# Merging two DMA transposes into one, moving four more transposes to DMA, and splitting the last eviction, in a fused recurrence and two-layer kernel

## The chip, the cores and the metric

The kernel runs on one core of a Trainium2 chip. The metric is the device time of one execution in microseconds (us). Three runs of the kernel before gave 184.88, 185.29 and 185.72 us, median 185.29 us. The profile was taken of a separate execution of 186.47 us, in which the span from the first to the last recorded instruction is 184.7 us.

Five engines are named as the profile names them: PE (matrix multiply, with PEld for its weight loads), DVE, ACT, POOL and SP. SP does no arithmetic. It issues most of the DMAs, one after another, in the order written in the program.

## The reference

Two steps follow one another. The first is a gated linear recurrence for 4 batches, 8 heads, 768 time steps and a head dimension of 48, the second is a two-layer network over the 3072 tokens that the first step gives.

```python
B, H, S, D = q.shape                     # 4, 8, 768, 48
for t in range(S):
    state = alpha[:, :, t, :, None] * state + np.einsum('bhd,bhe->bhde', k[:, :, t], v[:, :, t])
    y[:, :, t] = np.einsum('bhd,bhde->bhe', q[:, :, t], state)
x = y.transpose(0, 2, 1, 3).reshape(B * S, H * D)   # 3072 x 384
h = x @ w_in                             # 384 x 2048
g = np.maximum(h, 0.0) ** 2
out = g @ w_out                          # 2048 x 384
```

## The kernel before

**Tiling.** The 3072 tokens are cut into 24 chunks of 128 time steps, six for each batch. A chunk is a 128 x 384 tile of x once its recurrence is done. The chunks are numbered from 0, so chunk 14 is the 15th.

**Recurrence of a chunk.** The loop over time steps is replaced by matrix products inside a chunk and a state carried from chunk to chunk. For chunk s the steps are: the logarithm of alpha (`e_ln`, ACT); its running sums in two layouts (`e_p0` and `e_pT`, PE); exponentials of these (ACT); products of the exponentials with q and k (DVE); the scores (`e_p2`, PE); a mask (`e_sm`, DVE); the state update (`e_ps`, PE, and `e_stm`, `e_sb`); and the chunk's y in two parts (`e_p3a`, `e_p3b`, PE). `e_xn` (ACT, line 615) copies y out of PSUM as the bf16 tile `xn`.

**Two ways to transpose q and k.** Up to chunk 10 the products are transposed on PE. From chunk `RAW = 11` on, q and k themselves are cast to bf16 on POOL into `rawb` (`e_rb`, line 415) and transposed by a DMA into `rawt` (`e_turn`, line 418): one DMA for q and one for k. `e_qAT` (DVE, line 509) reads the q half of `rawt`, `e_kz` (line 513) the k half, and the scores need both. `rawb` and `rawt` have `NR = 3` slots.

**Two ways to transpose x.** The second step needs x with its columns on the partitions, in `xT_big`. `e_p4` (PE, three transposes) with `e_xT` (DVE copy, line 390 through `cast`) does it for most chunks. For chunks in `XTURN = (18, 23)`, that is 18 to 22, a DMA transposes `xn` straight into `xT_big` (`e_xt`, line 625). Chunk 23 goes through PE again.

**The two-layer step.** Groups of tokens (`GN`: 4, 1, 1, then two chunks each) go through `add_moe1` (x times w_in, relu on ACT, square on DVE) and `add_moe2` (times w_out, four quarters of four matmuls for each chunk). The first matmul of a pair such as chunks 14 and 15 reads `xT_big` of both. The result leaves PSUM by `e_ev` (ACT or DVE) and goes to memory by a DMA that SP issues, or for chunks 8 to 17 by one that POOL issues; chunks 0 to 7 are held and stored in two large DMAs late.

**What sets the order.** A planner (`Plan.run`) runs in Python while the program is built. Each piece of work is an `Op` with an engine, an assumed duration, a latency and what it depends on; the planner places them one by one and then emits the instructions in the order of the assumed starts. The order on every engine is therefore fixed in the program: PE, SP and POOL run their lists strictly one after another, and an instruction that must wait holds up all those behind it on the same engine. The planner's pseudo-engines "DMA", "TR" and "OUT" all become SP's one list: loads, transposes and stores. Its constants `LD1`, `TLD`, `TLAT`, `TLATE` say how long it assumes a load or a transpose to take. `gate` holds back the recurrence of chunk s until the two-layer step has come within `LEAD = 3.5` chunks of it.

**SP's list around the change.** Loads are written Q, K, V, A (for q, k, v, alpha), the q and k transposes Tq and Tk, the x transposes X, each with its chunk. Before the change the part that matters reads: Q12 Tq11 K12 Tk11 V12 A14 Tq12 Q13 K13 Tk12 V13 A15 Q14 Tq13 K14 Tk13 V14 A16 Q15 Tq14 K15 Tk14 V15 A17 Q16 Tq15 K16 Tk15 V16 A18 Tq16 Q17 Tk16 K17 V17 A19 Q18 Tq17 K18 Tk17 V18 Tq18 A20 Q19 Tk18 K19 V19 A21 Q20 Tq19 K20 Tk19 V20 Tq20 A22 Q21 Tk20 K21 X18 V21 A23 Tq21 Q22 Tk21 K22 V22 X19 Tq22 Q23 Tk22 K23 X20 V23 Tq23 Tk23 X21, two large stores, X22, and the last stores.

Lines that the steps touch:

Of the kernel before, what the change touches and what calls it, by code (L numbers as in the profile page):

```python
# [8 lines left out]
FP32 = mybir.dt.float32  # L9
# [45 lines left out]
def after(op, x=0.0):  # L55
    return (op, x)
# [85 lines left out]
def kernel(  # L142
# [10 lines left out]
    nc = tc.nc  # L153
    B, H, S, D = q.shape
    HD = H * D
    P = 128
# [3 lines left out]
    d_model, d_ff = moe_w_in.shape  # L160
# [3 lines left out]
    NT = n_tok // P  # L164
# [13 lines left out]
    opool = ctx.enter_context(tc.tile_pool(name="opool", bufs=6))  # L178
# [15 lines left out]
        out=utri_f, in_=utri_f, compare_op=ALU.is_ge, fill=0.0,  # L194
# [10 lines left out]
    for c in range(JN):  # L205
        blk = slice(JP * c, JP * c + JP)
        nc.gpsimd.affine_select(
            out=tri4[blk, 0:JW], in_=tri4[blk, 0:JW], compare_op=ALU.is_ge, fill=0.0,
# [27 lines left out]
    def pin(ins):  # L236
        tc.keep_in_program_order(ins)

    def mm(*a, **kw):
        pin(nc.tensor.matmul(*a, **kw))  # L240

    def tr(*a):
        pin(nc.tensor.transpose(*a))  # L243
# [13 lines left out]
    X_SLACK = 0.2  # L257
    LD = 0.98
    LD1 = 1.0
    WLD = 2.1  # L260
    LAG = 3.2
    SQ_PRIO = 0.0

    def add(eng, dur, emit, *deps, **kw):
        return plan.add(Op(eng, dur, emit, deps, **kw))
# [6 lines left out]
    def load_w(which):  # L272
# [25 lines left out]
        prev = w_cast[-SB] if len(w_cast) >= SB else None  # L298
        ld = add("DMA", WLD * n / 4 + 0.03, e_issue, prev, lat=LAG if which == "o" else 2.0)
        op = add({"POOL": 0.1 + 0.46 * n, "DVE": 0.1 + 0.2 * n, "ACT": 0.1 + 0.32 * n}, 0, e_cast, ld, prio=-3.0)  # L300
# [6 lines left out]
    C = [dict() for _ in range(NT)]  # L307
# [1 line left out]
    SRC = dict(srcs)  # L309
    EARLY = 4  # L310
    RAW = 11
    XTURN = (18, 23)
    TLD, TLAT, TLATE = 1.0, 4.0, 2.0
    NR = 3
    R = {}

# [49 lines left out]
    def add_load(s, nm):  # L366
        d = C[s]
        b, c = divmod(s, NCH)

        def ld():  # L370
            if nm not in d:
                d[nm] = loads.tile([P, H, D], FP32, name=nm)
            pin(nc.sync.dma_start(out=d[nm], in_=SRC[nm][b, c]))
        prev = C[s - LB].get("use_" + nm) if s >= LB else None
        d["ld_" + nm] = add("DMA", LD if s < 4 else LD1, ld, prev, lat=2.0 if s < 4 else LAG if s < 6 else 2.4, at=0.6)

    def add_chunk(s):
        d = C[s]
        b, c = divmod(s, NCH)
# [3 lines left out]
        g = dict(prio=-10.0 + s * 0.01)  # L383
# [26 lines left out]
        if raw:  # L410
            w, wz = s % NR, s % 2

            def e_rb(j, nm):
                raw_tiles()
                pin(nc.gpsimd.tensor_copy(R["b"][:, w, j, :, 0:D], d[nm]))  # L415

            def e_turn(j):
                pin(nc.sync.dma_start_transpose(out=R["t"][:, w, j], in_=R["b"][:, w, j].rearrange("p h d -> p (h d)")))
            rt = []
            for j, nm in enumerate(["qt", "kt"]):  # L420
                cb = add("POOL", 0.55, lambda j=j, nm=nm: e_rb(j, nm), d["ld_" + nm],
                         *([C[s - NR]["turn"][j]] if s >= RAW + NR else []), prio=-5.0)
                d["use_" + nm] = cb
                t_ = add("TR", TLD, lambda j=j: e_turn(j), cb, *([C[s - NR]["turned"][j]] if s >= RAW + NR else []), lat=TLAT)
                t_.late = TLATE
                rt.append(t_)
            d["turn"] = rt
        vb = d["use_vt"] = add("POOL", 0.55, e_vb, d["ld_vt"], old, prio=-5.0)

        def e_p0():  # L430
# [49 lines left out]
        if raw:  # L480
# [8 lines left out]
            aT = add("ACT", 0.48, e_AT, pT, after(ai) if ai else None, **g)  # L489
            aiT = add("ACT", 0.48, e_AiT, pT, after(aT), *([C[s - 2]["p2"]] if s >= RAW + 2 else []), **g)  # L490
# [20 lines left out]
        def e_kz(hh):  # L511
            rows = slice(DP * hh, DP * hh + DP)
            pin(nc.vector.tensor_mul(R["z"][rows, wz, :, hh, :], R["t"][rows, w, 1], R["i"][rows, wz]))  # L513
        if raw:
            if not last:
                mk = d["use_kt"] = add("DVE", 0.47, e_kI, ai, d["ld_kt"], old, **g)
            cp = add("DVE", 0.34, e_qAT, aT, rt[0], **g)
            prz = C[s - 2]["p2"] if s >= RAW + 2 else None
            kz0 = add("DVE", 0.45, lambda: e_kz(0), aiT, rt[1], prz, **g)
            kz1 = add("DVE", 0.45, lambda: e_kz(1), aiT, rt[1], prz, after(kz0), **g)  # L520
            d["turned"] = [cp, kz1]
            cpk = kz1
        else:
            mq = d["use_qt"] = add("DVE", 0.47, e_qA, a_, d["ld_qt"], old, **g)
            mk = d["use_kt"] = add("DVE", 0.47, e_kI, ai, d["ld_kt"], old, **g)
# [13 lines left out]
        def e_cp(lo, hi):  # L539
            if lo == 0:  # L540
                d["qkT"] = work.tile([P, 2 * NP, P], BF16, name="qkT")
            cast(cpk if lo else cp, d["qkT"][:, lo:hi, :], d["pT"][:, lo:hi, :])
        if s < EARLY:
            cp = add({"ACT": 0.49, "DVE": 0.34}, 0, lambda: e_cp(0, NP), p1q, **g)
            cpk = add({"DVE": 0.34, "ACT": 0.49}, 0, lambda: e_cp(NP, 2 * NP), p1k, after(cp, -9.0), **g)
        elif not raw:
            cp = cpk = add("DVE", 0.61, lambda: e_cp(0, 2 * NP), p1k, **g)
# [23 lines left out]
        if not last:  # L571
# [7 lines left out]
            prev = C[s - 1].get("sb") if s else None  # L579
            if c == 0 and s:  # L580
                prev = C[s - 2]["sb"]
# [34 lines left out]
        xn = add("ACT", 0.36, e_xn, p3b, **g)  # L616
        (p3a or p3b).gives = xn

        def e_p4():
            d["px"] = psum(p4, [P, KT, P], BF16)  # L620
            for j in range(KT):
                tr(d["px"][:, j, :], d["xn"][:, j * P:(j + 1) * P], ident_bf)
        if XTURN[0] <= s < XTURN[1]:
            def e_xt():
                pin(nc.sync.dma_start_transpose(out=xT_big[:, :, s * P:(s + 1) * P], in_=d["xn"]))
            d["x"] = add("TR", 0.8, e_xt, xn, lat=TLAT)
            d["x"].late = 1.0
            d["end"] = xn
            return
# [17 lines left out]
    OUT_LATE = 3.5  # L647
# [7 lines left out]
    prog = {"m1": 0.0, "m2": 0.0}  # L655
# [40 lines left out]
    def add_moe2(g, tt, before, box, quarters, pools):  # L696

        for qd in quarters:
            def e_mm(qd=qd):
                if qd == 0:  # L700
                    box["po"] = psum(box["first"], [P, 512], FP32)[:, 0:d_model]
                for kf in range(qd * FT // NQ, (qd + 1) * FT // NQ):
                    mm(box["po"], lhsT=gT[g][:, kf, tt * P:(tt + 1) * P], rhs=w_out_b[:, kf, :],
                       start=(kf == 0), stop=(kf == FT - 1))
            fs = range(qd * FT // NQ, (qd + 1) * FT // NQ) if g == 0 else range(FT)
            deps = [o for f in fs for o in sq[(g, f)]] + [w_dep("o", fs[-1] if g == 0 else FT - 1)] + ([after(before)] if before else [])
            op = plan.add(Op("PE", 0.65, e_mm, deps, takes=pools if qd == 0 else None, prio=0.1))
            op.moe = (2, 2.56 / NQ)
            if qd == 0:
                box["first"] = op  # L710
            op.lat = 0.05
            before = op
        if quarters[-1] < NQ - 1:
            return op

        t = GT[g] + tt
        held = t < HELD

        def e_ev():
            if held:  # L720
                if t % 4 == 0:
                    KEEP[t // 4] = stage.tile([P, 4, d_model], FP32, name="keep", tag="stage")
                box["ob"] = KEEP[t // 4][:, t % 4, :]
            else:
                box["ob"] = opool.tile([P, d_model], FP32, name="ob")
            if ev.eng == "DVE":
                pin(nc.vector.tensor_copy(box["ob"], box["po"]))
            else:
                pin(nc.scalar.copy(box["ob"], box["po"]))  # L729
        ev = add({"DVE": 0.47, "ACT": 0.38}, 0, e_ev, op, prio=-15.0)  # L730
        box["first"].gives = ev

        def e_held():
            pin(nc.sync.dma_start(out=out_r[t - 3:t + 1].rearrange("t p n -> p t n"), in_=KEEP[t // 4]))
        if held:
            held_ev.append(ev)
            if t % 4 == 3:
                add("OUT", 2.2, e_held, *held_ev[-4:], at=HELD_AT)
            return op

        def e_out():
            dma = nc.gpsimd if pool_out else nc.sync
            pin(dma.dma_start(out=out_r[GT[g] + tt], in_=box["ob"]))
        pool_out = POOL_OUT[0] <= GT[g] + tt < POOL_OUT[1]
        if pool_out:
            o = add("POOL", 1.0, e_out, ev, prio=5.0)
            o.late, o.moves = 0.5, 0.5
        else:
            add("OUT", 0.55, e_out, ev, at=0.0).late = OUT_LATE
        return op  # L750

    DMA_ORDER = ["at", (0, "qt"), (0, "kt"), (1, "qt"), (1, "kt"), (0, "vt"), (2, "qt"),
# [51 lines left out]
    LEAD = 3.5  # L804

    def gate(op):
        s = getattr(op, "gla", None)
        if s is not None:
            return s <= LEAD + (prog["m1"] + prog["m2"]) / 5.12
        return True  # L810

    def on_pick(op):
# [15 lines left out]
    for op in plan.order:  # L828
        if op.eng == "PE":
# [3 lines left out]
            if pe_end is not None and DUMMY and not opened and op.start < CALM:  # L833
                n = max(0, int((op.start - pe_end) / 0.11 + (0.4 if op.start < DENSE else -1.8)))
# [35 lines left out]
```

## Time and profile before

| what | value |
|---|---|
| median of three runs | 185.29 us |
| profiled execution, device time | 186.47 us |
| its span | 184.7 us |
| PE busy | 177.7 us, 96% of the span |
| DVE busy, ACT busy | 130.6 us, 126.7 us |
| DMA packets under 512 B | 112384 of 120056 |
| transposes by DMA: q and k, x | 26, 5 |
| transposes of xn on PE | 57 (19 chunks of 3) |

In the profile, "SPq" is SP's list. A line of the timeline gives the start, the duration and what was issued; a DMA's duration there is the time its issue took, not the time until its data arrived. "DMA to landing" is the time from issue to arrival. Line numbers are those of the kernel before; PE's lines are those of two helpers (240 for a matmul, 243 for a transpose), so its work is told apart by tiles.

### The profile page before, as it was taken

The page shows a single profiled execution, that of the slowest core. Times are in us where ns is not written, and L with a number is a line of the kernel's source. Part 1 is how long each engine was busy: PE and PEld are TensorE (multiplying, and loading weights), DVE is VectorE, ACT ScalarE, POOL GpSimd, SP SyncE. Part 2 cuts the span into 40 slices and gives each one's busy share as a digit, 9 for nine tenths or more (in the row PEclk, how much of TensorE's full clock was granted, in tenths as well). Part 3 has the DMA queues.
Part 4 walks back from the last instruction along what each step waited for, and adds up shares of the span by engine and source line. Part 5 has one row for each costly group of instructions (what it writes and reads, how often), then busy time and mean ns, then how long its engine had stood idle before and what let it go on. Part 6 is the DMA issues. An engine that isn't in the chain of part 4 may idle for free.

```text
span 184.7 us, 4919 instructions
## 1 busy us (share of the span) xinstructions
PE 177.7 (96%) x1886; PEld 133.5 (72%) x1886; DVE 130.6 (71%) x283; ACT 126.7 (69%) x288; POOL 41.8 (23%) x81
## 2 busy tenths in 40 slices
PE   7798999999999999999999999999999999999992
PEld 2467795467868887977867867868876877978661
DVE  1248898965899998776878877868866786845100
ACT  3657699606867996958958958958965975848221
POOL 8121100011161134142224242243243311000000
PEclk9969999999999999999999999999999999999999
DMA  5999999999989888989999899999999967601112
GB/s 167 215 216 243 270 367 331 324 233 214 209 169 218 171 173 165 177 155 172 154 168 205 158 196 177 237 186 155 220 164 205 207 97 248 202 4 43 41 47 85
DMA packets 120056, 34.12 MB, mean 185 GB/s; under 512 B 112384, under 2 KB 118784, under 8 KB 120032
## 3 DMA queue, kind: packets, MB, share of 16 engines
q1 hardware_dynamic: 119392, 31.83, 83.6%
q0 software_dynamic: 640, 1.97, 3.1%
q8 instruction: 15, 0.25, 0.6%
q14 instruction: 9, 0.07, 0.2%
HBM read 25.17 MB, written 4.72 MB: 162 GB/s over the span
## 4 chain that ended last, share of the span: by engine, by line
PE 88%; ACT 6%; DMA 2%; issue 1%; DVE 1%; SPq 0%; ACTq 0%
PE bank L240 76%; PE sc L240 5%; PE bank L243 5%; ACT r L681 3%; DMA at<-in_alpha_dram 2%; PE st L240 2%; DVE w_out_b L295 1%; ACT A L464 0%; ACT gT L343 0%; ACT xn L388 0%; ACT Ainv L468 0%; ACT w_in_b L297 0%; ACT qkT L388 0%; ACT L_s L398 0%; ACT ob L729 0%
## 5 line engine op out<-in xcount | busy, mean ns | idle before, releaser
L240 PE MATMUL bank<-xT_big,w_in_b 128*128 128x256 bf16 (+2 forms) x636 | 73.6, 262 | 0.1
L240 PE MATMUL bank<-w_out_b,gT 128*128 128x384 bf16 x384 | 71.1, 326 | 0.5 <-DVE w_out_b L295 0.5
L681 ACT ACTIVATE r<-bank 128x512 bf16<-128x512 f32 x96 | 55.9, 618 | 7.3 <-PE bank L240 6.2
L240 PEld LDWEIGHTS <-w_in_b 128*128 128x128 bf16 x636 | 53.3, 98 | 8.0 <-issue 0.2
L240 PEld LDWEIGHTS <-gT 128*128 128x128 bf16 x400 | 36.0, 98 | 20.1 <-DVE w_out_b L295 1.0
L689 DVE TENSOR_TENSOR gT<-r 128x512 bf16<-128x512 bf16 x96 | 40.9, 455 | 9.6 <-ACT r L681 8.8
L566 DVE TENSOR_TENSOR sm<-sc,utri_b 128x512 bf16<-128x512 f32 x48 | 30.8, 684 | 5.9 <-PE sc L240 5.7
L407 POOL CAST vb<-vt 128x384 bf16<-128x384 f32 x24 | 13.5, 561 | 65.6 <-DMA vt<-in_v_dram 52.2
L729 ACT COPY ob<-bank 128x384 f32<-128x384 f32 x16 | 7.7, 478 | 19.1 <-PE bank L240 18.8
L507 DVE TENSOR_TENSOR kI_s<-kt,Ainv 128x384 bf16<-128x384 f32 x21 | 12.4, 591 | 7.3 <-ACT Ainv L468 7.3
L388 ACT CAST xn<-bank 128x384 bf16<-128x384 f32 x24 | 11.5, 479 | 8.3 <-PE bank L240 8.3
L415 POOL CAST rawb<-qt 128x384 bf16<-128x384 f32 x13 | 8.0, 614 | 19.8 <-DMA qt<-in_q_dram 15.7
L591 ACT CAST sb<-st 128x384 bf16<-128x384 f32 x20 | 9.7, 484 | 3.8 <-DVE st L586 3.6
L586 DVE TENSOR_TENSOR st<-st,ae_s 128x384 f32<-128x384 f32 x20 | 11.2, 559 | 1.5 <-ACT ob L729 0.5
L513 DVE TENSOR_TENSOR kz<-rawt,kz 64x512 bf16<-64x512 bf16 x26 | 11.5, 441 | 1.1 <-ACT kz L456 0.4
L415 POOL CAST rawb<-kt 128x384 bf16<-128x384 f32 x13 | 7.9, 607 | 17.7 <-DMA kt<-in_k_dram 16.5
L240 PE MATMUL bank<-warm 128*128 128x256 bf16 (+1 forms) x48 | 10.5, 356 | 1.3 <-DVE warm L188 1.3
L504 DVE TENSOR_TENSOR qA_s<-qt,A 128x384 bf16<-128x384 f32 x11 | 6.1, 551 | 7.7 <-ACT A L464 7.7
L398 ACT ACTIVATE L_s<-at 128x384 bf16<-128x384 f32 x20 | 10.6, 530 | 0.2
L468 ACT ACTIVATE Ainv<-bank 128x384 bf16<-128x384 f32 x21 | 10.6, 503 | 0.0
L240 PEld LDWEIGHTS <-qkT 64*128 64x128 bf16 (+1 forms) x168 | 7.9, 96 | 3.1 <-issue 0.8
L240 PEld LDWEIGHTS <-sm 128*128 128x128 bf16 x192 | 8.2, 96 | 1.5 <-DVE sm L566 0.2
(65 smaller groups left out, 181.4 us busy)
## 6 DMA issues: line engine op xcount, KB each, us to landing
qt<-in_q_dram SPq DMA_DIRECT2D x24, 192.0 KB, 4.1
kt<-in_k_dram SPq DMA_DIRECT2D x24, 192.0 KB, 3.7
vt<-in_v_dram SPq DMA_DIRECT2D x24, 192.0 KB, 3.8
at<-in_alpha_dram SPq DMA_DIRECT2D x20, 192.0 KB, 3.9
wo<-in_moe_w_out_dram SPq DMA_DIRECT2D x4, 768.0 KB, 8.3
out_dram<-ob POOLq DMA_DIRECT2D x10, 192.0 KB, 3.6
wi<-in_moe_w_in_dram SPq DMA_DIRECT2D x4, 384.0 KB, 5.4
wi<-in_moe_w_in_dram SPq DMA_DIRECT2D x2, 768.0 KB, 7.9
```

The lines of the kernel that those rows point to most:

```text
L240: pin(nc.tensor.matmul(*a, **kw))
L388: pin(nc.scalar.copy(out_t, in_t))
L398: pin(nc.scalar.activation(L[:, :, 0:D], d["at"], AF.Ln))
L407: pin(nc.gpsimd.tensor_copy(d["vb"], d["vt"]))
L415: pin(nc.gpsimd.tensor_copy(R["b"][:, w, j, :, 0:D], d[nm]))
L468: pin(nc.scalar.activation(d["Ai"], d["pm"][:, 0:HD].rearrange("p (h d) -> p h d", h=H), AF.Exp, scale=-1.0))
L507: pin(nc.vector.tensor_mul(kI[:, :, 0:D], d["kt"], d["Ai"]))
L513: pin(nc.vector.tensor_mul(R["z"][rows, wz, :, hh, :], R["t"][rows, w, 1], R["i"][rows, wz]))
L566: pin(nc.vector.tensor_mul(d["sm"][:, hh], d["sc"][:, hh], utri_b.to_broadcast([P, NP, P])))
L586: pin(nc.vector.tensor_mul(st4, st4, bcast(ae, D)))
L681: pin(nc.scalar.activation(box["r"][:, 0:w], box["ph"][:, 0:w], AF.Relu))
L689: pin(nc.vector.tensor_mul(gT[g][:, f0:f0 + per, lo * P:lo * P + n], r, r))
```

## The change

Four things change.

1. `e_turn` no longer takes a chunk's q and k one by one. A single DMA transposes both, 128 x 1024 elements in place of two of 128 x 512. It depends on both casts, and everything that read one half of `rawt` now depends on it. 26 such DMAs become 13.
2. `XTURN` becomes (14, 23): x of chunks 14, 15, 16 and 17 is transposed by DMA too, in place of three PE transposes and one DVE copy each.
3. The planner's constants change: `LD2 = 0.93` for loads from chunk 11 on, `TLD`, `TLAT`, `TLATE`, and the assumed time of an x transpose. `gate` lets the recurrence run up to half a chunk further ahead from chunk 13 on. These change the order only.
4. The last tile's result is copied out of PSUM by DVE (left half) and ACT (right half), and its store waits for both.

SP's list becomes: Q12 K12 T11 V12 A14 Q13 T12 K13 V13 A15 Q14 K14 T13 V14 A16 Q15 T14 K15 V15 A17 Q16 K16 T15 V16 A18 Q17 T16 K17 V17 A19 Q18 T17 K18 X14 V18 A20 Q19 K19 T18 V19 X15 A21 Q20 T19 K20 V20 X16 A22 Q21 T20 K21 V21 X17 A23 Q22 K22 T21 V22 Q23 K23 X18 V23 T22 X19 T23 X20 X21, a large store, X22, the other large store, and the last stores.

```diff
+    LD2 = 0.93
-    XTURN = (18, 23)
-    TLD, TLAT, TLATE = 1.0, 4.0, 2.0
+    XTURN = (14, 23)
+    TLD, TLAT, TLATE = 1.2, 4.5, 1.5
...
-        d["ld_" + nm] = add("DMA", LD if s < 4 else LD1, ld, prev, lat=2.0 if s < 4 else LAG if s < 6 else 2.4, at=0.6)
+        d["ld_" + nm] = add("DMA", LD if s < 4 else LD1 if s < RAW else LD2, ld, prev, lat=2.0 if s < 4 else LAG if s < 6 else 2.4, at=0.6)
...
-            def e_turn(j):
-                pin(nc.sync.dma_start_transpose(out=R["t"][:, w, j], in_=R["b"][:, w, j].rearrange("p h d -> p (h d)")))
+            def e_turn():
+                pin(nc.sync.dma_start_transpose(
+                    out=R["t"][:, w].rearrange("p j n t -> p (j n) t"), in_=R["b"][:, w].rearrange("p j h d -> p (j h d)")))
             rt = []
             for j, nm in enumerate(["qt", "kt"]):
                 cb = add("POOL", 0.55, lambda j=j, nm=nm: e_rb(j, nm), d["ld_" + nm],
-                         *([C[s - NR]["turn"][j]] if s >= RAW + NR else []), prio=-5.0)
+                         C[s - NR]["turn"] if s >= RAW + NR else None, prio=-5.0)
                 d["use_" + nm] = cb
-                t_ = add("TR", TLD, lambda j=j: e_turn(j), cb, *([C[s - NR]["turned"][j]] if s >= RAW + NR else []), lat=TLAT)
-                t_.late = TLATE
-                rt.append(t_)
-            d["turn"] = rt
+                rt.append(cb)
+            d["turn"] = turn = add("TR", TLD, e_turn, *rt, *(C[s - NR]["turned"] if s >= RAW + NR else []), lat=TLAT)
+            turn.late = TLATE
...
-            d["x"] = add("TR", 0.8, e_xt, xn, lat=TLAT)
+            d["x"] = add("TR", 0.6, e_xt, xn, lat=TLAT)
...
+        def e_half(eng, lo, hi):
+            if eng == "DVE":
+                box["ob"] = opool.tile([P, d_model], FP32, name="ob")
+                pin(nc.vector.tensor_copy(box["ob"][:, lo:hi], box["po"][:, lo:hi]))
+            else:
+                pin(nc.scalar.copy(box["ob"][:, lo:hi], box["po"][:, lo:hi]))
+        half = None
+        if t == NT - 1:
+            half = add("DVE", 0.26, lambda: e_half("DVE", 0, d_model // 2), op, prio=-15.0)
+            ev = add("ACT", 0.22, lambda: e_half("ACT", d_model // 2, d_model), op, after(half, -9.0), prio=-15.0)
+        else:
+            ev = add({"DVE": 0.47, "ACT": 0.38}, 0, e_ev, op, prio=-15.0)
...
-            return s <= LEAD + (prog["m1"] + prog["m2"]) / 5.12
+            return s <= LEAD + min(0.5, max(0.0, 0.25 * (s - 12))) + (prog["m1"] + prog["m2"]) / 5.12
```

## The prediction

> **What bounds the kernel now.** I read the page's busy shares first, then the busy time by stage, then SP's timeline, then the answers on the tiles that the change touches, and last the end of the chain.
>
> ```profile
> PE 177.7 (96%) x1886; PEld 133.5 (72%) x1886; DVE 130.6 (71%) x283; ACT 126.7 (69%) x288; POOL 41.8 (23%) x81
> ...
> 80.00:100.00 20.00, 20.00 (x204) 15.04 (x202) 15.54 (x33) 14.71 (x36) 6.16 (x11) 1.00 1.06 172
> 100.00:120.00 20.00, 20.00 (x219) 16.42 (x218) 16.64 (x37) 16.30 (x39) 6.32 (x11) 1.00 1.07 194
> ```
>
> In the stage rows the first pair after the window is its length and PE's busy time. From 80 to 120 us PE does not rest, and DVE and ACT have a fifth of their time free. So only less work on PE, or a shorter end, can make this kernel faster, and any wait that reaches PE is paid in full. The last two columns say that the DMA engines are busy too (share 1.06 and 1.07). The second view is SP's list in time, start and duration of each issue.
>
> ```profile
> 81.40 1.34 SPq L418 DMA_TRANSPOSE rawt<-rawb  x1
> 82.83 0.54 SPq L373 DMA_DIRECT2D kt<-in_k_dram  x1
> 83.47 1.22 SPq L418 DMA_TRANSPOSE rawt<-rawb  x1
> 84.74 0.57 SPq L373 DMA_DIRECT2D vt<-in_v_dram  x1
> 85.41 0.55 SPq L373 DMA_DIRECT2D at<-in_alpha_dram  x1
> 86.05 0.79 SPq L373 DMA_DIRECT2D qt<-in_q_dram  x1
> 86.94 1.50 SPq L418 DMA_TRANSPOSE rawt<-rawb  x1
> ...
> 117.14 0.57 SPq L373 DMA_DIRECT2D vt<-in_v_dram  x1
> ```
>
> Each issue starts within 0.05 to 0.1 us of the end of the one before it: SP has no rest. It feeds the recurrence at its own pace and runs only a little ahead of PE. What it delivers, and when, is in the next two answers (x transposes, then q and k transposes).
>
> ```profile
> L625 SPq DMA_TRANSPOSE xT_big<-xn x5: 1207/1352/1963, 130.3 to 157.6; - x5
> DMA to landing us min/median/max: 2.3/3.5/4.9
> ...
> L418 SPq DMA_TRANSPOSE rawt<-rawb x26: 1189/1269/2650, 68.6 to 147.9; - x26
> DMA to landing us min/median/max: 2.6/3.3/5.2
> ```
>
> The first matmuls of chunks 14 and 15 in the two-layer step, which the change makes depend on DMAs, stand here:
>
> ```profile
> 113.21 0.82 PE L240 MATMUL bank<-xT_big,w_in_b 128*128 128x256 bf16 x6
> ```
>
> **What the change takes off PE.** Four chunks lose their three transposes. The chain shows three such matmuls at 0.17 us, so 4 x 0.17 = 0.67 us go, all on the path. The four DVE copies of 0.35 us that go with them lie beside PE's work: 0.
>
> **The end.** The last copy is 128x384 on ACT, 0.48 us, with nothing beside it. A 128x512 relu takes 0.618 us and this copy 0.478, so 128 elements cost 0.14 us and half a row on ACT about 0.27. DVE's own copy of the whole is 0.558 us, so its half, the later one, takes about 0.31. The gain is 0.48 - 0.31 = 0.17 us, between 0 (SP's second wait, or both engines slowed on one PSUM tile) and 0.24. I take 0.17.
>
> **The longer lead.** It adds no instruction. PE's new order brings the sums of chunks 14 and later about 3 us earlier. The transposes of q and k must be there by then: now DVE starts to use k 4.4 to 8.1 us after it landed. In the new list T14 stands where Tq14 stood at 86.94, less what three merged pairs save, and lands by about 92; its reader moves from 99.0 to about 95.9. A margin of 4 us covers it: 0. The loads behind X14 to X17 are late by a few us, but their readers stand ten or more us away: 0. On POOL the first store moves behind chunk 17's q cast; six output buffers, one used every 3.3 us, cover that: 0.
>
> **What the merge gives to SP's list.** Let d be the saving for a chunk. Before, a chunk is transpose, one load, transpose, three loads: 2.07 (81.40 to 83.47) + 3.47 (83.47 to 86.94) = 5.54 us. After, it is one transpose and four loads. One single transpose with four loads takes 4.38 us (102.98 to 107.36 in the same timeline), and the merged one moves twice the bytes, so d is at most 1.16. If it takes as long as two, d is 0; were the issue itself twice as long with the engines idle meanwhile, d would be somewhat below 0. Between these: loads alone on a full list run at 0.90 us for 192 KB (60.98 to 66.37, six of them). At that rate 256 KB of transpose take 1.20, and with four loads 4.80, so d = 0.74; or 4.38 plus 0.60 for the second half make 4.98, d = 0.56. I take 0.65, as the share of over 1.0 says that bytes, not issues, set the pace.
>
> **What the four x transposes cost.** Each stands in the same list. One takes 0.45 us by bytes (96 KB) and 1.3 by its issue; I take 0.8.
>
> **When X15 arrives.** Before X15, SP's new list holds the loads up to V19, T11 to T18, and X14. The old list has got through these loads and transposes at 117.7 (V19 starts at 117.14). So SP reaches X15 at 117.7 + 0.8 - 8d = 118.5 - 8d, with d = 0.65 at 113.3. Its `xn` is long there: the cast of chunk 15 ends at 110.6 now and moves 2.8 us earlier. With the median 3.5 us to landing, x is there at 116.8. On PE the first matmul of chunks 14 and 15 stands at 113.21 now; in the new order chunk 16's scores and outputs and chunk 17's sums come before it (1.04 us more), two PE transposes less (0.34): 113.9. PE then has nothing else it may do. **It waits 2.9 us, in general 8.1 - 8d.**
>
> **When X17 arrives.** The old list has the loads up to V21, its transposes up to chunk 20 and one x transpose behind it at 132.1; the new one adds two more x transposes: 133.7 - 10d. With 3.5 us that is 130.7. The first matmul of chunks 16 and 17 (126.49 now) moves to 126.6, plus the 2.9 already lost: 129.5. Another 1.2 us, in general 2.5 - 2d.
>
> **X19 and X21** find SP's list run down: X19's turn comes at about 137.6, just before its `xn` (138.02 now, 4.1 earlier in the new order, 4.1 later by the waits), and its matmul at 143.9. No wait.
>
> **The sum.** Waits 10.6 - 10d = 4.1 us, less 0.67, less 0.17: +3.3 us. The profiled execution of 186.47 us (span 184.7, 1.8 around it) would become 189.8; it stood 1.18 us above the median, so against 185.29 I forecast **188.6 us**.
>
> **A rule against it.** The granted clock was 0.61 from 8 to 12 us, where the span has its one slow stretch, and 1.00 in every stage after 13 us, through PE waits of under 1.5 us. The Trainium skill, "TensorE: Matmul & The Clock Gate", Part 1, says that one idle window of about 3.4 us halves the clock until PE has been busy for as long. By the row the sum stands; by the rule a wait over 3.4 us (d under 0.59) would cost up to 1.7 us more, an estimate from that page.
>
> **Rivals.**
> - *Nothing is late (the other side).* One mechanism: SP's pace. If d is 1.01 or more, X15 lands by 113.9 and both waits vanish. That is a merged DMA costing hardly more than a single one. For it: x transposes of 96 KB and q transposes of 128 KB have the same shortest issue, 1.207 and 1.189 us, so issue does not grow with size. Against: the DMA share over 1.0, and 0.90 us for a load whose shortest issue is 0.52. Time: 185.29 - 0.84 = 184.4. The skill's "DMA: Bandwidth & Descriptors", Rules for kernel authors, says to coalesce many small transfers, as under 64 KB they are mostly overhead; these are of 128 KB, so by it too most of a transpose is transfer.
> - *The waits are small.* d of 0.8 to 1.0: x is late by under 2 us in all; 184.6 to 187, and most of it under 186.2.
> - *The merge saves nothing.* d = 0: waits 10.6, time 185.29 + 10.6 - 0.84 = 195.0. It needs an issue of some 2.4 us. Against: the equal shortest issues above.
> - *The merged transpose itself is late* for DVE: margin 4 us above, against 0.6 us more transfer. I give it no time.
>
> **How the numbers follow.** The forecast, d from 0.4 to 0.85, has 0.55 and its own range, 186.5 to 191.0; small waits 0.10; nothing late 0.27; nothing saved 0.08. The range goes from 184.2, just under the second side, to 193.0 (d = 0.2), and leaves out 0.1. A measurement of this kernel can tell about 0.5%, 0.93 us. Nothing late gives 0.84, with its spread on both sides of that bound: 0.18 faster, 0.09 same; small waits give 0.08 same and 0.02 slower; all else is slower, 0.65.
>
> **What would show it.** In the profile after: the issue of line 419, one per chunk, near 1.2 us with landing near 4; SP's list still without rest to 130 us; X15 issued near 113 while its `xn` was done near 108; a PE wait put down to the DMA `xT_big<-xn`, some 3 us near 114 and 1 us near 130; PE's transposes 45 in place of 57; the last two copies near 0.3 us side by side. The prediction is wrong if SP waits for `xn` at X15 (then d was over 1.0), if a wait for `rawt` shows on DVE, or if the merged issue is twice as long.

## The result, and the profile after

The changed kernel took 190.91 us (median of six runs, 190.28 to 193.21), the kernel before 185.32 us in the same comparison (184.88 to 186.37): 1.0285 times as long, 95% interval 1.0249 to 1.0322, so 5.6 us slower by the medians. One of the six runs, 193.21 us, lies over 1.5% above the fastest and is not in the ratio; the ratio alone gives 5.3 us. The profiled execution after took 190.28 us, its span is 188.6 us.

The same views as before, first the busy shares and the stages (in a stage row: the window, its length and PE's busy time, the other engines' busy times, then the granted clock, the DMA engines' share and GB/s):

```profile
PE 176.8 (94%) x1873; PEld 132.5 (70%) x1874; DVE 129.5 (69%) x280; ACT 126.8 (67%) x288; POOL 40.7 (22%) x81
```

```profile
80.00:100.00 20.00, 20.00 (x220) 15.59 (x218) 16.66 (x36) 15.05 (x37) 7.15 (x13) 1.00 1.04 199
100.00:120.00 20.00, 16.97 (x159) 12.85 (x157) 12.36 (x26) 13.68 (x33) 7.50 (x13) 0.92 1.07 208
```

From 80 to 100 us nothing has changed: PE is busy throughout. From 100 to 120 us it now rests for 3.0 us, and its clock is 0.92 on average. SP's list (timeline) and PE's list at that place show why:

```profile
108.11 1.01 SPq L374 DMA_DIRECT2D kt<-in_k_dram  x1
109.23 1.70 SPq L419 DMA_TRANSPOSE rawt<-rawb  x1
110.97 0.60 SPq L374 DMA_DIRECT2D vt<-in_v_dram  x1
111.67 2.20 SPq L626 DMA_TRANSPOSE xT_big<-xn  x1
113.92 0.58 SPq L374 DMA_DIRECT2D at<-in_alpha_dram  x1
```

```profile
112.71 0.36 PE L240 MATMUL bank<-vb,sm 128*128 128x48 bf16 x8
116.11 0.71 PE L240 MATMUL bank<-xT_big,w_in_b 128*128 128x256 bf16 x5 [3.03 <-DMA xT_big<-xn]
```

The transpose at 111.67 is X15. Its `xn` had been ready since 107.1 us; for 4.5 us it stood in SP's list, behind Q19, K19, the merged T18 and V19. It landed at 116.06, and until then PE's next matmul, the first of chunks 14 and 15, had to wait: 3.03 us. The answers on the transposes:

```profile
L626 SPq DMA_TRANSPOSE xT_big<-xn x9: 1181/1203/2204, 104.7 to 158.2; - x9
DMA to landing us min/median/max: 2.3/3.3/4.7
...
L419 SPq DMA_TRANSPOSE rawt<-rawb x13: 1244/1696/2968, 69.8 to 141.1; - x13
DMA to landing us min/median/max: 3.6/4.1/5.6
```

Merged or single, the shortest issue is the same (1.24 and 1.19 us), and the median has grown from 1.27 to 1.70 us for twice the bytes. Then the clock, in stage rows of PE's wait and of what follows it:

```profile
112.90:116.10 3.20, 0.17 (x7) 0.08 (x4) 1.27 (x3) 1.48 (x4) 1.21 (x3) 1.00 0.92 165
113.50:116.90 3.40, 0.80 (x8) 0.71 (x8) 1.27 (x3) 0.88 (x3) 1.08 (x2) 1.00 0.97 179
116.90:120.30 3.40, 3.40 (x19) 2.42 (x17) 1.14 (x3) 2.11 (x4) 0.51 (x1) 0.51 1.17 231
120.30:125.00 4.70, 4.70 (x56) 4.03 (x55) 3.13 (x8) 3.66 (x9) 1.07 (x3) 0.99 1.05 189
```

0.8 us after PE had resumed, its clock was halved for 3.4 us. Half of that, 1.7 us, is lost. Last the end of the timeline, first before, then after:

```profile
180.50 0.81 PE L240 MATMUL bank<-w_out_b,gT 128*128 128x384 bf16 x4
...
181.35 0.48 ACT L729 COPY ob<-bank 128x384 f32<-128x384 f32 x1 [2.12 <-PE bank L240]
```

```profile
183.79 0.65 PE L240 MATMUL bank<-w_out_b,gT 128*128 128x384 bf16 x3
...
184.48 0.36 DVE L734 COPY ob<-bank 128x192 f32<-128x192 f32 x1 [11.95 <-PE bank L240]
184.87 0.32 ACT L736 COPY ob<-bank 128x192 f32<-128x192 f32 x1 [2.52 <-DVE ob L734]
```

The two halves do not run side by side. ACT waits for DVE's half, and the two end 0.75 us after PE's last matmul, where before the single copy ended after 0.51 us. The rest of the end, from the last copy to the last instruction, is longer too, by 0.54 us (3.39 against 2.84); that is not the split, as run 1 below has 3.37 with one copy.

**Where the time went.** The two spans differ by 3.9 us. Cut at the first matmul `bank<-utri_b,L_s` of chunk 11 and at PE's last matmul:

| stretch | before | after | difference |
|---|---|---|---|
| start to the first such matmul | 76.08 | 75.42 | -0.66 |
| from there to PE's last matmul | 105.24 | 109.02 | +3.78 |
| PE's last matmul to the end | 3.36 | 4.14 | +0.78 |

The middle row is the wait (3.03), the halved clock (1.67) and the 12 transposes less (-0.67), together 4.03; the other 0.25 us are not assigned (PE rested for only 0.05 us in that stretch before, so it was not lost waits). In the first row the profile before has its slow stretch at 8 to 12 us, that after has none. This is one reason why the medians lie further apart than the two profiles: the profiled execution stood 1.2 us above its median before, 0.6 us below it after, and the two differ by 3.8 us: 3.8 + 1.2 + 0.6 = 5.6.

### The profile page after: what moved, and what is told of

Its sections match the earlier page's. It is cut to its first block, busy times and chain, and to the rows that moved or that the text cites. A ratio compares the mean times of both kernels' runs of the same rounds, so it can differ in the third digit from the quotient of the medians.

```text
span 188.6 us, 4865 instructions
## 1 busy us (share of the span) xinstructions
PE 176.8 (94%) x1873; PEld 132.5 (70%) x1874; DVE 129.5 (69%) x280; ACT 126.8 (67%) x288; POOL 40.7 (22%) x81
## 4 chain that ended last, share of the span: by engine, by line
PE 83%; ACT 6%; DMA 5%; DVE 2%; issue 2%; SPq 0%; ACTq 0%
PE bank L240 73%; PE sc L240 5%; PE bank L243 4%; ACT r L682 3%; DMA xT_big<-xn 2%; DMA at<-in_alpha_dram 2%; PE st L240 2%; DVE w_out_b L296 1%; ACT A L465 0%; DVE gT L690 0%; DVE qA_s L505 0%; ACT gT L344 0%; ACT sb L592 0%; ACT xn L389 0%; ACT Ainv L469 0%
## 5 line engine op out<-in xcount | busy, mean ns | idle before, releaser
L240 PE MATMUL bank<-xT_big,w_in_b 128*128 128x256 bf16 (+2 forms) x635 | 75.1, 266 | 3.2 <-DMA xT_big<-xn 3.0
L240 PE MATMUL bank<-w_out_b,gT 128*128 128x384 bf16 x384 | 69.9, 326 | 0.5 <-DVE w_out_b L296 0.5
L240 PEld LDWEIGHTS <-w_in_b 128*128 128x128 bf16 x636 | 54.2, 99 | 12.0 <-issue 3.3
L690 DVE TENSOR_TENSOR gT<-r 128x512 bf16<-128x512 bf16 x96 | 39.3, 436 | 15.4 <-ACT r L682 14.6
L514 DVE TENSOR_TENSOR kz<-rawt,kz 64x512 bf16<-64x512 bf16 x26 | 12.2, 469 | 1.7 <-ACT kz L457 0.9
L505 DVE TENSOR_TENSOR qA_s<-qt,A 128x384 bf16<-128x384 f32 x11 | 6.9, 628 | 7.6 <-ACT A L465 7.6
L416 POOL CAST rawb<-qt 128x384 bf16<-128x384 f32 x13 | 7.0, 539 | 22.8 <-DMA qt<-in_q_dram 22.8
L240 PE MATMUL bank<-warm 128*128 128x256 bf16 (+1 forms) x48 | 9.3, 325 | 1.3 <-DVE warm L188 1.3
L755 POOL DMA_DIRECT2D out_dram<-ob x10 | 5.6, 556 | 16.1 <-ACT ob L730 14.8
```

What stands on the lines that cost most here:

```text
L690: pin(nc.vector.tensor_mul(gT[g][:, f0:f0 + per, lo * P:lo * P + n], r, r))
```

## The experiments

Theory: what costs the time is X15's place in SP's list, behind T18 and V19, and the halved clock behind its wait. Rivals: the merged transpose or the new order costs by itself; the longer lead brings the wait about; the split end costs.

The kernels are the changed kernel with one edit, unless another base is named. The kernel before took 184.95 and 184.94 us in the two groups of the first eight runs, on one chip, and 185.88 us on the chip of the last two. The middle stretch is the second row of the table above.

**1. The last tile in one copy.** The split alone is undone.

```diff
-        if t == NT - 1:
+        if t == NT:
```

> The changed kernel, but the last tile leaves PSUM in one ACT copy as before. My theory of the whole loss of 5.6 us: PE waits 3.2 us for the DMA transpose of x of chunk 15; the clock is halved behind that wait, 1.7 us; the two halves of the last copy run one after the other and the end is 0.8 us longer; the twelve transposes gone give back 0.7. So here: about 190.91 - 0.8 = 190.1 us. Rival: the split gains as it was meant to (0.17 us), and the longer end in the one profile is chance: 191.1 us.

Measured: 186.74 us, 1.0085 [1.0052, 1.0119], and not 190.1. The chain is the same, with other sizes (PE's waits; us in total, times, longest):

```profile
PE bank L240 <- DMA xT_big<-xn: 3.1, 2, 2.3
```

X15 was issued at 109.48, its `xn` ready since 106.05, and landed at 114.32. The wait was 2.3 us, a second one for X17 0.8 us, and the clock stayed whole. No edit of the end can do that, so the changed kernel had to run again on this chip (5).

**2. PE kept busy in the gap.** 28 matmuls of constant data, 128 x 256 each, stand ahead of the first matmul of chunks 14 and 15, written into the PSUM tile that the real ones then overwrite.

```diff
+                    if GT[g] == 14 and f == 0:
+                        for _ in range(28):
+                            mm(box["ph"][:, 0:256], lhsT=warm[:, 0:P], rhs=warm[:, 0:256], start=True, stop=True)
```

> The changed kernel with 28 more matmuls of 128x256 on constant data, which PE runs just ahead of the first matmul of chunks 14 and 15, that is inside the wait; their result is overwritten. My theory: the matmuls take 3.05 us of a wait of 3.2, so they cost next to nothing, and the granted clock stays at 1.00 behind the wait: 190.91 - 1.7 = 189.2 us. Rival: the matmuls from 117 to 120 us ran at half pace because of something else (the DMAs that landed then, or x arriving in pieces); then they stay slow, and the time is 190.9 or more.

Measured: 187.69 us (187.39 to 188.4), 1.0139 [1.0105, 1.0172]. In PE's timeline the added matmuls fill the gap:

```profile
111.95 3.22 PE L240 MATMUL bank<-warm 128*128 128x256 bf16 x28
115.01 2.24 PE L240 MATMUL bank<-xT_big,w_in_b 128*128 128x256 bf16 x19
```

PE was busy from 112 to 120 us at a clock of 1.00. The 189.2 us that I expected were reckoned from 190.91, and the changed kernel was faster on this chip (5): against it this run is 0.5 us lower, with overlapping intervals. None of its four executions has a mean clock under 0.996, while two of four in run 5 have 0.991. That fits the theory, but with four executions each it is a weak test.

**3. No x transposes more.** X goes by DMA from chunk 18 as before; merge, lead and split stay.

```diff
-    XTURN = (14, 23)
+    XTURN = (18, 23)
```

> The changed kernel with x by DMA only for chunks 18 to 22, as before the change; the merged transposes, the longer lead and the split last copy stay. My theory: no wait of PE for x, no halved clock, four chunks of PE transposes back (0.67 us), the longer end stays: about 185.3 + 0.8 = 186.1 us. Rival: the merge or the longer lead itself costs (transposes of q and k late, or a worse order on PE): then it stays above 188 us.

Measured: 185.29 us, 1.0009 [0.9989, 1.003]. No PE wait on `xT_big` is left, and the loss is gone: the four x transposes bring it, and merge, lead and split together cost at most 0.3%. I had expected 186.1: the end is 0.53 us longer than before in this profile, but the middle stretch is 0.53 us shorter (104.71), for no reason that I can name.

**4. X15 earlier in SP's list, all else as in 1.** With a longer assumed load the planner places X15 ahead of Q19, T18, K19 and V19. X14, X16 and X17 move forward by four places too, so this run tests the place of all four.

```diff
-    LD2 = 0.93
+    LD2 = 1.05
...
-        if t == NT - 1:
+        if t == NT:
```

> The changed kernel with one number of the planner raised, the assumed time of a load from 0.93 to 1.05, and the last copy in one piece. In SP's list X15 then stands behind A20, ahead of Q19, T18, K19 and V19, and X14 ahead of A19, Q18, T17 and K18. My theory: X15 is issued some 4 us earlier, near 108, lands before 113, PE does not wait: 185.3 - 0.7 = 184.6 us. Rival: what is late is the transfer, not the place in the list (4.4 us from issue to landing on busy DMA engines), and the loads set behind X15 are then late themselves: a wait stays, 187 us or more.

Measured: 185.33 us (184.02 to 186.3, 12 runs), 1.0006 [0.9979, 1.0032]. SP's timeline:

```profile
105.67 1.43 SPq L374 DMA_DIRECT2D at<-in_alpha_dram  x1
107.20 1.32 SPq L626 DMA_TRANSPOSE xT_big<-xn  x1
108.57 0.58 SPq L374 DMA_DIRECT2D qt<-in_q_dram  x1
```

X15 is issued 0.7 us after its `xn` (106.52), lands at 110.04, and PE starts on it at 112.30 without a wait:

```profile
112.30 2.38 PE L240 MATMUL bank<-xT_big,w_in_b 128*128 128x256 bf16 x20
```

The middle stretch is 104.52 us against 105.24 before, about the 0.67 of the saved transposes. So the place decides: with the same four transposes and the same merged DMAs, but each x transpose four places earlier, the loss is gone. The median is about 1 us over the profiled execution (184.4) and not under the kernel before, where I had expected 184.6; which wait the other executions have is not known.

**5. The changed kernel again, on this chip.**

> The changed kernel once more, beside the others of this group. With one last copy (the run before) it took 1.0085 of the kernel before, with waits of 2.4 and 1.0 us for x and the clock never halved; the change itself took 1.0285, with one wait of 3.0 us and the clock halved behind it. My theory now: one copy more or less at the very end cannot change the waits, so the two differ by how long the wait was in that group of runs, and by the halved clock that comes only with the longer one. If the waits here are near 2.5 us and the clock stays whole: about 1.013 (the waits of 3.4, the longer end of 0.5 to 0.8, less 0.67, make +2.4 to 2.9 us); if they are near 3.2 us, 1.025 to 1.03. Rival: the split last copy is worth 4 us by itself; then 1.025 or more with waits near 2.5 us.

Measured: 188.18 us, 1.0162 [1.0121, 1.0202], between the two cases that I had named. PE's waits and its timeline at the place:

```profile
PE bank L240 <- DMA xT_big<-xn: 2.5, 2, 2.0
```

```profile
114.48 1.69 PE L240 MATMUL bank<-xT_big,w_in_b 128*128 128x256 bf16 x14 [1.96 <-DMA xT_big<-xn]
```

The same waits, 2.0 and 0.5 us in place of 3.03. In the profiled execution the clock was 1.000; of the four, two have a mean clock of 0.997 or more and took 187.36 and 187.84 us, two have 0.991 and took 188.51 and 188.99. In the comparison of the result all six had 0.981 to 0.991. So with waits of this length an execution sometimes pays for a halved clock too and sometimes not, which is 1 to 2 us; only the first of the four was profiled. What decides it is taken up under the clock below.

**6. The merge alone.** The kernel before with the merged transpose and the changed constants for it; no x transposes more, no lead, one copy. The edit is the `e_turn` part of the diff above, with `LD1` kept for all loads.

> The kernel before with the merged transposes and the planner's numbers of the change, without the four more x transposes, the longer lead and the split copy. PE has the same work as before. My theory: the merge shortens SP's list by 0.7 to 1.1 us a chunk (T to T with four loads between near 5.0 us in place of 5.54, and fewer stops behind a full list), nothing waits for it, and the time is that of before within 0.3%: 184.6 to 185.4 us. Rival: the merge itself costs (its larger transfer holds up the loads behind it, or PE's order is worse): over 186 us.

Measured: 186.06 us, 1.0051 [1.0033, 1.007], a loss where I expected none. PE's timeline has a stall in chunk 22 that the kernel before has not:

```profile
150.69 0.65 PE L240 MATMUL bank<-w_out_b,gT 128*128 128x384 bf16 x3
151.74 0.23 PE L240 MATMUL sc<-qkT,kz 128*128 128x128 bf16 x1 [0.40 <-DVE kz L514]
152.19 0.28 PE L240 MATMUL sc<-qkT,kz 128*128 128x128 bf16 x2 [0.23 <-DVE kz L514]
```

By the starts of the matmuls 0.96 us is lost there, and the middle stretch is 0.85 us longer. Here `rawt` of chunk 22 had landed 15 us before DVE used it; DVE comes to it late: its list has four other operations ahead from 149.41 us on, the first of which had waited 0.78 us for ACT. So the stall comes with the order that the planner makes of the new numbers; run 3, which has the merge too but also the lead, `LD2` and the split, does not have it. The merged DMA itself keeps PE waiting nowhere.

**7. The split alone.** The kernel before with the last tile in two halves, by the `e_half` part of the diff.

> The kernel before with nothing but the last copy split between DVE and ACT. My theory from the profile after: ACT starts when DVE is done (0.36 and then 0.32 us in place of one copy of 0.48), and the store goes out 0.2 us later; end behind PE 3.6 to 4.1 us in place of 3.4: +0.2 to +0.7 us, 185.2 to 185.7. What the prediction had said: 0.17 us faster.

Measured: 185.10 us, 1.0004 [0.9985, 1.0022].

```profile
179.40 0.36 DVE L733 COPY ob<-bank 128x192 f32<-128x192 f32 x1 [9.35 <-PE bank L240]
179.79 0.32 ACT L735 COPY ob<-bank 128x192 f32<-128x192 f32 x1 [2.51 <-DVE ob L733]
```

The halves run in series here too: 0.74 us from PE's end to the last copy's end, 0.23 more than the single copy. That is below what the times can show.

**8. X14 and X16 by DMA, 15 and 17 through PE,** in one copy, so that each pair of chunks has only its earlier one on SP's list.

```diff
-        if XTURN[0] <= s < XTURN[1]:
+        if s in (14, 16) or 18 <= s < XTURN[1]:
...
-        if t == NT - 1:
+        if t == NT:
```

> The changed kernel with one last copy, and x by DMA for chunks 14 and 16 but not for 15 and 17, which go through PE again. Of a pair of chunks that the two-layer step reads together, the even one is done some 7 us before the odd one, so its transpose has that much longer. My theory: PE waits for no x, half of the PE transposes stay away (0.34 us): 184.95 - 0.34 = 184.6 us. Rival: SP's list is too full for any more x transposes; then X14 or X16 holds up what is behind it and a wait for x, rawt or a load appears on PE: 186 us or more.

Measured: 184.83 us, 0.9989 [0.9963, 1.0015]. One PE wait of 0.2 us on `xT_big` is left, for X19. It is the fastest of all medians, but the interval takes in no change, and what it could gain, six PE transposes, is 0.34 us.

**9. Without the longer lead.** The recorded expectation says that this kernel has one copy at the end. It was run with the two halves, so it is to be read against the changed kernel and not against 1.

```diff
-            return s <= LEAD + min(0.5, max(0.0, 0.25 * (s - 12))) + (prog["m1"] + prog["m2"]) / 5.12
+            return s <= LEAD + 0.0 + (prog["m1"] + prog["m2"]) / 5.12
```

> The changed kernel without the longer lead, and with the last tile in one copy, so that it differs from the run with one copy by the lead alone. Its DMA list puts X15 behind Q20 and K20, three loads later than there (109.48 us), so it should be issued near 112.2 and land, 4.3 us later, near 116.5. Without the lead PE comes to the first matmul of chunks 14 and 15 near 111.1. My theory, that the lead is worth something because the planner also moves X15 with it: one wait of about 5.4 us, behind which the clock is halved for 3.4 us (1.7 us more): 184.95 + 5.4 + 1.7 - 0.67 = 191.4 us. If even such a wait leaves the clock whole: 189.7. The prediction's step, that the lead costs and brings nothing: as the run with one copy, 186.7.

Measured: 191.26 us, 1.0237 [1.015, 1.0324]. The sum came out as I had it (191.4), by luck, as its parts did not:

```profile
113.39 1.84 SPq L374 DMA_DIRECT2D kt<-in_k_dram  x1
115.34 2.55 SPq L626 DMA_TRANSPOSE xT_big<-xn  x1
```

```profile
116.29 0.81 PE L240 MATMUL bank<-w_out_b,gT 128*128 128x384 bf16 x4
120.54 0.72 PE L240 MATMUL bank<-xT_big,w_in_b 128*128 128x256 bf16 x5 [3.44 <-DMA xT_big<-xn]
```

```profile
118.38:121.80 3.42, 1.26 (x12) 1.14 (x13) 0.42 (x1) 0.40 (x1) 1.88 (x4) 1.00 0.90 145
121.80:125.20 3.40, 3.40 (x21) 2.35 (x19) 1.12 (x3) 0.80 (x2) 0.16 (x1) 0.50 0.86 204
```

X15 is issued 3.7 us later than in the changed kernel's profile, but PE comes to its matmul about 4 us later too: the wait is 3.44 us, not 5.4. The clock is halved behind it, from 1.3 us after PE resumed (the last row is that stage). Its interval holds both readings of the changed kernel (1.0285 and 1.0162, on other chips or in other groups), so the lead by itself has no effect that these runs show. It moves X15 and the matmul by about as much.

**10. The merge alone undone.** The kernel before with x by DMA from chunk 14 and the longer lead; q and k by two DMAs, one copy.

```diff
-    XTURN = (18, 23)
+    XTURN = (14, 23)
...
-            d["x"] = add("TR", 0.8, e_xt, xn, lat=TLAT)
+            d["x"] = add("TR", 0.6, e_xt, xn, lat=TLAT)
...
-            return s <= LEAD + (prog["m1"] + prog["m2"]) / 5.12
+            return s <= LEAD + min(0.5, max(0.0, 0.25 * (s - 12))) + (prog["m1"] + prog["m2"]) / 5.12
```

> The kernel before with x by DMA from chunk 14 and the longer lead, but with q and k transposed by two DMAs as before, and one last copy: the merge alone is undone. The planner then puts X15 behind Tk17 and ahead of K18, not behind V19. By the list of the kernel before it is issued near 111.3 on that profile's clock and lands near 115.3, and the matmul stands near 113.9: one wait of about 1.5 us, and X17 in time. Theory that the place in the list decides and not the merge: 184.95 + 1.5 - 0.67 = 185.8 us, no more than the changed kernel with one copy (186.7). Rival, the prediction's case that without a saving by the merge x is late by 8.1 us and again by 2.5: 194 us.

Measured: 190.24 us, 1.0184 [1.0067, 1.0301]: neither 185.8 nor 194. PE's waits:

```profile
PE bank L240 <- DMA xT_big<-xn: 1.9, 2, 1.7
PE bank L240 <- ACT Ainv L468: 1.4, 2, 1.0
...
PE bank L240 <- DVE sm L566: 0.5, 2, 0.3
```

The place of X15 did what I had expected: issued at 110.86, a wait of 1.7 us for an expected 1.5. But without the merge the list stays long. Q12 to the end of V19 takes 53.1 us with three x transposes in it, 49.5 without these; part of the lateness is then paid by other loads, above all by one of alpha, which costs PE 0.96 us:

```profile
131.37 0.58 SPq L373 DMA_DIRECT2D at<-in_alpha_dram  x1
...
135.07 0.52 ACT L398 ACTIVATE L_s<-at 128x384 bf16<-128x384 f32 x1 [1.27 <-DMA at<-in_alpha_dram]
...
136.51 0.38 PE L240 MATMUL bank<-utri_b,L_s 128*128 128x128 bf16 x4 [0.96 <-ACT Ainv L468]
```

The transposes of q and k, never within 3.2 us of being late in the changed kernel, are down to a spare 0.1 to 0.8 us in chunks 19 to 22. So the merge does make the room that the x transposes use. With it, and the x transposes moved forward (4), nothing is lost. Without it X15 stands even further forward, ahead of K18, and lands too late all the same, other data come late as well, and 1.8% is lost.

## Why the prediction was right, and where its steps were not

The sign and the mechanism came out as forecast: X15 late behind SP's list, one PE wait of some 3 us (2.9 predicted, 3.03 measured) on the DMA `xT_big<-xn`. Experiments 3 and 4 show that this is the cause. The time was 2.3 us above the forecast of 188.6 and just inside that forecast's own range, which ends at 191.0. Of the 2.3 us only 0.5 lie between the profiled execution after (190.28) and the 189.8 that the sum gave for it; the other 1.8 are the 1.2 and 0.6 us by which the two profiled executions stood off their medians. That the sum came so near is in part luck, as the points show:

- **PE's transposes less, -0.67.** Right: 45 in place of 57, and the middle stretch of run 4, which waits for nothing there, is 0.72 us shorter than before.
- **The merge's saving d, taken as 0.65.** Mis-sized. Q12 to the end of V19 took 51.3 us before (49.6 in run 7) and, with the merge and without the time of X14's issue, 42.5 us in the changed kernel, 41.2 to 43.7 in runs 1, 3, 5, 6 and 9. Over eight chunks d is about 1.0 (0.7 to 1.3), 1.1 by the two main profiles. My argument that bytes set the pace fell: twice the bytes cost 0.4 us more of issue at the median, 0.05 at the shortest. With it falls what I held against the first rival, that most of a transpose of 128 KB is transfer: in SP's list it is not.
- **X15 reached at 118.5 - 8d.** The rule gave 113.3 with the wrong d, 109.7 with 1.1; measured 111.67. The anchor was wrong: I took the start of the list from one profile. Q12 was issued 9.7 us ahead of the first `bank<-utri_b,L_s` there, 7.6 us ahead of it after (first before, then after):

```profile
66.37 2.14 SPq L373 DMA_DIRECT2D qt<-in_q_dram  x1
```

```profile
67.83 0.55 SPq L374 DMA_DIRECT2D qt<-in_q_dram  x1
```

That puts 2.1 us back, X14 took 1.2 instead of 0.8, and X15's landing 4.4 instead of 3.5. From 8.1 - 8d = -0.7 these three make 2.7. Of the other 0.3, about half is the matmul's own place, which came 0.16 us earlier than the step had it; the rest lies in the rounding of d and in the list itself.
- So the wait came out right by luck, by errors that cancel, and **the rival "nothing is late" was misjudged.** Its own condition, d of 1.01 or more, was about met; the kernel waited all the same. What I called one mechanism, SP's pace, were two: the pace, and where the list stands when it begins. A point from which it decides must carry the spread of all its terms.
- **X17, a second wait of 1.2.** None in the profile after (landed 128.23, needed at 130.41, after the lost time); 0.8 and 0.5 us in runs 1 and 5, where the first wait was shorter. The step's 2.5 - 2d gives 0.3. Right in kind, too large by about what d was off.
- **The end, -0.17.** Wrong in sign: +0.24 us in the changed kernel, +0.23 in run 7. The step that failed is "its half, the later one, takes about 0.31": I took the halves as side by side, and they run in series. The Trainium skill, "PSUM — Partial Sum Buffer", section "PSUM bank collisions raise a hardware error", says that a compiler back end lets no two engines touch one bank in the same quadrant at once, ACT and DVE included. The trace agrees so far as every profile with the split (after, runs 2, 3, 5, 7 and 9) has ACT start 0.03 us after DVE's half has ended. It does not show whether the shared PSUM tile makes ACT wait or the result tile `ob`, of which the two also write one half each; the profile only puts ACT's wait down to DVE's copy. The halves were also longer than the step had them, 0.36 and 0.32 us against 0.31 and 0.27.
- **The longer lead, 0.** Holds within what run 9 can tell.
- **The merged transpose itself late: no time.** Right; the smallest spare time of `rawt` after was 3.2 us against the 4 us of the step.
- **The clock.** I left it out of the sum and gave 1.7 us for waits over 3.4 us. The price was right, the point was not: the clock was halved behind 3.03 us (and 3.44 in run 9), and stayed whole behind 2.3, 2.0 and 1.7 us. This is the largest of the terms that the sum lacked. The Trainium skill, "TensorE: Matmul & The Clock Gate", has two figures for it: an idle window of about 3.4 us in Part 1, and no gap over some 3 us in "Why this matters for your kernels". The five waits agree with the second, but the length of a wait does not tell all.
- **Where a wait falls.** The Trainium skill says in the same Part 1 that the window runs freely. The traces agree: in run 9 the clock falls at 9.16 and again at 121.80 us, and the 112.64 us between are 33.0 times the 3.413 us that a slow stretch lasts; in every profile the time from one change of the clock to the next is a whole number of such windows, and where the first begins differs from run to run. Counted in these windows, PE rested for 2.6 us of the window ahead of the drop in the changed kernel (the row from 113.50), and for 2.15 us in run 9 (118.38 to 121.80), where the 3.44 us fell into two windows. In runs 1, 5 and 10, with the windows counted back from the drop of the clock after the last instruction, the one with the most rest had 1.67, 1.83 and 1.73 us, and the clock stayed whole. The slow stretch at the start does not follow this: in the profile before the clock fell behind a window with 1.0 us of rest. So a wait of 2 to 3 us may halve the clock or not, by where it falls. That fits two of four executions of run 5 losing clock, which is argued and not shown, as those two were not profiled.

With the measured terms the sum against the profiled execution is 3.03 + 1.67 - 0.67 + 0.24 = +4.3, against the +3.9 of the spans. What the sum leaves out are the start (-0.66), the rest of the end (+0.54) and the 0.25 us not assigned.

Open: why in the first comparison all six runs lost clock, by their mean clocks, and on the second chip two of four. No run has two result tiles or two PSUM tiles, one for each half, so what makes the halves run in series stays open as well.

## What to carry to other kernels

In this kernel a transfer's lateness was decided by its place in the issuing list and by the list's pace, so look at what stands ahead of it there before asking how fast it is: moving the x transposes four places forward undid a loss of 0.9% (runs 1 and 4). Where work is moved from the bounding engine to a list without rest, make room on that list first, and leave a margin of some microseconds, since the same entry of this list, Q12, stood 7.3 to 9.7 us ahead of chunk 11's first `bank<-utri_b,L_s` in these profiles. A PE wait of about 3 us can cost more than its length, here 1.7 us more.

## What the runs showed of the hardware

- The clock was halved for 3.4 us after PE waits of 3.03 and 3.44 us, beginning 0.8 and 1.3 us after PE had resumed; not after the profiled waits of 2.3 us or less. In the middle of the kernel it fell where PE had rested for 2.15 us or more of one window of 3.413 us, and not where it had rested for 1.83 or less.
- A DMA transpose of 256 KB in SBUF was issued in about as little time as one of 128 KB (1.24 and 1.19 us at the shortest); the median from issue to landing rose from 3.3 to 4.1 us.
- Most issues of SP's list took 0.55 to 1.9 us, but in every profile some took 2.0 us or more, up to 3.65 (a transpose of k in run 7); X15 itself took 2.20 us after and 1.21 in run 1. This moves the whole list behind it.
- Copies of two halves of one PSUM tile by DVE and ACT ran one after the other in each of the profiles that have them.
